# Attention and SwiGLU FFN on one core: Q and K by DMA transpose, weights over SP and Pool, matmuls in column tiles

## The chip, the cores and the metric

The kernel runs on one core of a Trainium2 chip. The core has five engines that run side by side and meet at semaphores: PE (matmuls), DVE (vector operations), ACT (activation functions and copies), POOL (GpSimd) and SP (which here only issues DMAs). DMA transfers are issued from the queue of an engine and run on 16 DMA engines. Matmul results land in PSUM, all other tiles in SBUF. The metric is device time of one execution, in microseconds, as the median of several runs.

## The reference, cut to what matters

Inputs are `q`, `k`, `v` of shape (8 batches, 12 heads, 448 positions, 64), the weights `w_gate` and `w_val` (768, 1536), `w_out` (1536, 768) and `rms_g` (768), all float32.

```python
scores = (q @ k.T) / sqrt(64)                 # per batch and head
attn   = maximum(scores, 0.0) ** 2 / 448
x      = (attn @ v)                           # heads side by side: (3584, 768)
rms = sqrt(mean(x * x, axis=-1) + 1e-06)
xn  = x / rms * rms_g
out = (silu(xn @ w_gate) * (xn @ w_val)) @ w_out
```

There is no softmax: a score is clipped at zero and squared, so nothing has to be summed over a row before the product with V.

## The kernel before, in words

Everything on PE is bfloat16 with float32 sums. All weights stay in SBUF. One batch of 448 positions is the unit of work, and the kernel keeps two in flight: while the FFN of batch b runs, the attention of batch b+1 is threaded into it.

Loading. Q, K and V of a batch come with the positions in four chunks of 112 partitions, cast from float32 to bfloat16 by the DMA itself, issued on POOL (`load`, L90). The weights come the same way (`load_w` L100, `load_wo` L107), behind the first batch's loads on the same queue.

Attention works on pairs of heads (`HP` = 6 pairs a batch). `transposes` (L154): DVE copies the pair's Q and K into order (`reorder`, L148, two copies), PE transposes eight 112x128 blocks into a PSUM tile `psT` (L163), and DVE copies that to SBUF as `qkT` (L169). `scores` (L182) multiplies, for each chunk of 112 keys, the two heads of the pair in two row tiles of the array (64 rows each); ACT clips at zero (L197), on every fourth chunk DVE (L195), and DVE squares (L198). `attend` (L207) multiplies the squares by V, the two heads of the pair into the two column halves of the array; ACT scales into `xT` (L215), DVE squares that into `x2` (L218). `psT` and `psAV` share one PSUM buffer.

The norm (`norm`, L235 to L255) sums `x2` over the features with a matmul by ones (`psSS`, L238), takes the square root on ACT (L243, another function table than Silu's), the reciprocal on DVE (L246), and multiplies six tiles of `xn` on DVE (L249).

The FFN (`ffn`, L305) of a batch has 12 blocks of 128 hidden features; each is a `gate` and a `value` unit of six 128x128 matmuls over 448 columns (L260), with Silu on ACT (L271) and the product `hT` on DVE (L277). Two batches together make seven tiles of 128 rows of output (`outproj`, L286): three at the end of an even batch, four at the end of an odd one, each in a part of 512 and a part of 256 columns, copied to SBUF by ACT (L293) and stored from SP (L300).

The order on every engine is the order in which the program issues, written out by hand: `merge` (L18) spreads the attention's units and the norm evenly over the first nine tenths of the FFN's units, by the weights that stand beside them. The first attention and norm run with nothing beside them. The last batch's FFN has no attention in it.

Of the kernel before, what the change touches and what calls it, by code (L numbers as in the profile page):

```python
# [8 lines left out]
FP32 = mybir.dt.float32  # L9
I32 = mybir.dt.int32  # L10
# [7 lines left out]
def merge(main, side, head=0.0, tail=0.0):  # L18


    total = sum(c for c, _ in main)
    if not main:
        return [f for _, f in side]
    out, done, k = [], 0.0, 0
    n = len(side)
    for c, f in main:
        while k < n and done >= total * (head + (1.0 - head - tail) * k / n):
            out.append(side[k][1])
            k += 1
        out.append(f)  # L30
        done += c
    out.extend(f for _, f in side[k:])
    return out
# [3 lines left out]
def kernel(  # L37
# [22 lines left out]
    NT = 2 * S // P  # L60

    ctx.enter_context(tc.manual_schedule())

    const = ctx.enter_context(tc.tile_pool(name="consts", bufs=1))
    wpool = ctx.enter_context(tc.tile_pool(name="weights", bufs=1))
    ldpool = ctx.enter_context(tc.tile_pool(name="ld", bufs=2))
    tpool = ctx.enter_context(tc.tile_pool(name="tsb", bufs=2))
    apool = ctx.enter_context(tc.tile_pool(name="attn", bufs=10))
    xpool = ctx.enter_context(tc.tile_pool(name="xT", bufs=2))
    npool = ctx.enter_context(tc.tile_pool(name="norm", bufs=2))  # L70
    hpool = ctx.enter_context(tc.tile_pool(name="hT", bufs=2))
    spool = ctx.enter_context(tc.tile_pool(name="sig", bufs=3))
    opool = ctx.enter_context(tc.tile_pool(name="ostage", bufs=3))
    ps_s = ctx.enter_context(tc.tile_pool(name="ps_s", bufs=2, space=bass.MemoryType.PSUM))
    ps_a = ctx.enter_context(tc.tile_pool(name="ps_a", bufs=1, space=bass.MemoryType.PSUM))
    ps_m = ctx.enter_context(tc.tile_pool(name="ps_m", bufs=3, space=bass.MemoryType.PSUM))
# [7 lines left out]
    def alloc_ld(b):  # L84
        for nm in ("q", "k", "v"):
            ld[nm, b] = ldpool.tile([PC, H, NCH * D], BF16, name=nm + "b", tag=nm + "b")

    def load(nm, b, h0=0, h1=H):
        src = {"q": q, "k": k, "v": v}[nm]
        nc.gpsimd.dma_start(out=ld[nm, b][:, h0:h1, :], in_=head_rows(src, b, h0, h1))  # L90
# [4 lines left out]
    NSL = 4  # L95
    FS = F // NSL

    def load_w(which, s):
        dst, src = {"g": (wg_sb, moe_w_gate), "v": (wv_sb, moe_w_val)}[which]
        nc.gpsimd.dma_start(  # L100
            out=dst[:, :, s * FS : (s + 1) * FS],
            in_=src.rearrange("(kt p) f -> p kt f", p=P)[:, :, s * FS : (s + 1) * FS],
        )

    def load_wo(s, n):
        w = FT // n
        nc.gpsimd.dma_start(  # L107
            out=wo_sb[:, s * w : (s + 1) * w, :],
            in_=moe_w_out.rearrange("(fk p) m -> p fk m", p=P)[:, s * w : (s + 1) * w, :],
        )  # L110

    alloc_ld(0)
    load("q", 0, 0, 2)
    load("k", 0, 0, 2)
    ident = const.tile([PC, PC], BF16, name="ident", tag="ident")
    masks.make_identity(nc, ident[:])
    ones_bf = const.tile([P, P], BF16, name="ones_bf", tag="ones_bf")
    nc.vector.memset(ones_bf[:], 1.0)
    eps_col = const.tile([P, 1], FP32, name="eps_col", tag="eps_col")
    nc.vector.memset(eps_col[:], eps)  # L120
    g_sb = wpool.tile([P, KT], FP32, name="g_sb", tag="rmsg")
    nc.sync.dma_start(out=g_sb[:], in_=moe_rms_g.rearrange("(kt p) -> p kt", p=P))
    load("q", 0, 2, 6)
    load("k", 0, 2, 6)
    load("v", 0, 0, 6)
    load("q", 0, 6, 12)
    load("k", 0, 6, 12)
    load("v", 0, 6, 12)
    for s in range(NSL):
        load_w("g", s)  # L130
        load_w("v", s)
        if s == 1:
            alloc_ld(1)
            load("q", 1)
            load("k", 1)
    load("v", 1)
    load_wo(0, 2)
    load_wo(1, 2)


    xTs = {}
    qkT = {}
    ldp = {}

    def reorder(b, j):
        for nm in ("q", "k"):
            t = tpool.tile([PC, NCH, 2, D], BF16, name=nm + "p", tag=nm + "p")
            nc.vector.tensor_copy(  # L148
                out=t[:].rearrange("p c h d -> p h c d"),
                in_=ld[nm, b][:, 2 * j : 2 * j + 2, :].rearrange("p h (c d) -> p h c d", c=NCH),  # L150
            )
            ldp[nm, b, j] = t

    def transposes(b, j):  # L154
        if j == 0:
            xTs[b] = xpool.tile([P, KT, S], BF16, name="xT", tag="xT")
            reorder(b, 0)
        if j + 1 < HP:
            reorder(b, j + 1)
        psT = ps_a.tile([P, 2, S], BF16, name="psT", tag="ps_a")  # L160
        for ti, nm in enumerate(("q", "k")):
            for c in range(NCH):
                nc.tensor.transpose(  # L163
                    out=psT[:, ti, c * PC : (c + 1) * PC],
                    in_=ldp[nm, b, j][:, c, :, :],
                    identity=ident[:],
                )
        t = tpool.tile([P, 2, S], BF16, name="qkT", tag="qkT")
        nc.vector.tensor_copy(out=t[:], in_=psT[:])  # L169
        qkT[b, j] = t  # L170

    rsq = {}
    state = {"n": 0}

    def scores(b, j, cs):
        t = qkT[b, j]
        pss = []
        for c in cs:
            psS = ps_s.tile([PC, 2, 512], FP32, name="psS", tag="psS")
            for hh in range(2):  # L180
                prt = slice(hh * D, (hh + 1) * D)
                nc.tensor.matmul(  # L182
                    out=psS[:, hh, :S],
                    lhsT=t[prt, 1, c * PC : (c + 1) * PC],
                    rhs=t[prt, 0, :],
                    start=True,
                    stop=True,
                )
            pss.append(psS)
        for c, psS in zip(cs, pss):  # L190
            r = apool.tile([PC, 2, S], BF16, name="r", tag="r")
            on_dve = state["n"] % 4 == 3
            state["n"] += 1
            if on_dve:
                nc.vector.tensor_relu(out=r[:], in_=psS[:, :, :S])  # L195
            else:
                nc.scalar.activation(out=r[:], in_=psS[:, :, :S], func=ACT.Relu)  # L197
            nc.vector.tensor_tensor(out=r[:], in0=r[:], in1=r[:], op=ALU.mult)  # L198
            rsq[b, j, c] = r

    x2s = {}

    def attend(b, j):
        psAV = ps_a.tile([P, S], FP32, name="psAV", tag="ps_a")
        for c in range(NCH):
            for hh in range(2):
# [6 lines left out]
                )  # L213
        xT = xTs[b]
        nc.scalar.mul(out=xT[:, j, :], in_=psAV[:], mul=inv_attn)  # L215
        if j == 0:
            x2s[b] = npool.tile([P, KT, S], BF16, name="x2", tag="x2")
        nc.vector.tensor_tensor(out=x2s[b][:, j, :], in0=xT[:, j, :], in1=xT[:, j, :], op=ALU.mult)  # L218

    def attention(b):  # L220
        units = [(0.4, lambda: transposes(b, 0))]
        for j in range(HP):
            units.append((0.5, lambda j=j: scores(b, j, (0, 1))))
            if j + 1 < HP:
                units.append((0.4, lambda j=j: transposes(b, j + 1)))
            units.append((0.5, lambda j=j: scores(b, j, (2, 3))))
            if j:
                units.append((0.8, lambda j=j: attend(b, j - 1)))
        units.append((0.8, lambda: attend(b, HP - 1)))
# [3 lines left out]
    xns, hTs = {}, {}  # L233

    def norm(b):  # L235
        psSS = ps_m.tile([P, S], FP32, name="psSS", tag="mm")
        for kt in range(KT):
            nc.tensor.matmul(  # L238
                out=psSS[:], lhsT=ones_bf[:], rhs=x2s[b][:, kt, :],
                start=(kt == 0), stop=(kt == KT - 1),  # L240
            )
        rstd = npool.tile([P, S], FP32, name="rstd", tag="rstd", bufs=1)
# [4 lines left out]
        xn = npool.tile([P, KT, S], BF16, name="xn", tag="xn")  # L247
        for kt in range(KT):
            nc.vector.scalar_tensor_tensor(  # L249
                out=xn[:, kt, :], in0=xTs[b][:, kt, :], scalar=g_sb[:, kt : kt + 1], in1=rstd[:],  # L250
                op0=ALU.mult, op1=ALU.mult,
            )
        xns[b] = xn
        if b % 2 == 0:
            hTs[b // 2] = hpool.tile([P, FT, 2 * S], BF16, name="hT", tag="hT")  # L255

    def project(w_sb, b, fb, nm):
        ps = ps_m.tile([P, S], FP32, name=nm, tag="mm")
        for kt in range(KT):
            nc.tensor.matmul(  # L260
                out=ps[:], lhsT=w_sb[:, kt, fb * P : (fb + 1) * P], rhs=xns[b][:, kt, :],
                start=(kt == 0), stop=(kt == KT - 1),
            )
# [10 lines left out]
    def value(b, fb):  # L274
# [3 lines left out]
            out=hTs[b // 2][:, fb, o : o + S], in0=sil[b, fb][:], in1=psV[:], op=ALU.mult  # L278
# [4 lines left out]
    def outproj(i, t, o, w):  # L283
        ps = ps_m.tile([P, 512], FP32, name="psO", tag="mm")
        for fk in range(FT):
            nc.tensor.matmul(  # L286
                out=ps[:, :w], lhsT=hTs[i][:, fk, t * P : (t + 1) * P], rhs=wo_sb[:, fk, o : o + w],
                start=(fk == 0), stop=(fk == FT - 1),
# [69 lines left out]
```

## Time and profile before

| | us |
|---|---|
| median of 3 runs (lowest, highest) | 548.66 (547.95, 550.68) |
| the profiled execution: span from its first to its last instruction | 544.9 |
| busy in it: PE, DVE, ACT, POOL | 485.1, 338.6, 252.3, 34.4 |

The profile is of one execution, and its own time is known as this span; the runs' median lies 3.8 us above it, which is what lies around the first and the last instruction. Busy times of PE include the modelled drain of a matmul, so two matmuls that follow each other overlap in it: what a matmul costs in a stream is read from the distance between starts.

### The profile page before, as it was taken

What the parts mean: (1) busy time and instruction counts of PE and PEld (TensorE: products, weight loads), DVE (VectorE), ACT (ScalarE), POOL (GpSimd) and SP (SyncE); (2) the same over time, 40 slices, a digit from 0 to 9 for tenths busy, and PEclk for the clock granted to TensorE, in tenths of its full rate; (3) what the DMA queues carried; (4) which work ended last, traced back from release to release, by engine and by line L of the source; (5) the groups of instructions that cost most, each with busy time, mean ns of one, the idle gap of its engine ahead of it and who ended that gap; (6) DMA issues with size and microseconds to landing.
All of it is one profiled execution on the core that took longest, in us unless ns stands there. A gap on an engine that the chain in (4) does not pass through costs nothing.

```text
span 544.9 us, 7394 instructions
## 1 busy us (share of the span) xinstructions
PE 485.1 (89%) x3024; PEld 236.1 (43%) x3024; DVE 338.6 (62%) x586; ACT 252.3 (46%) x369; POOL 34.4 (6%) x45
## 2 busy tenths in 40 slices
PE   3774999879999799888999799987999899989996
PEld 1331444434444344444444444444445444444553
DVE  3886677467764677566774677656775677745210
ACT  2553454524545354535444454454545445553221
POOL 7330001000010001000010000100000000000000
PEclk9976999979999899999999999999999999999999
DMA  9999938150073402560054500733001200002013
GB/s 114 201 201 205 203 53 102 35 103 1 1 102 73 95 1 24 79 123 16 1 75 86 108 1 1 103 58 80 1 1 29 78 10 2 1 29 59 0 30 88
DMA packets 45858, 35.08 MB, mean 64 GB/s; under 512 B 2304, under 2 KB 42240, under 8 KB 45824
## 3 DMA queue, kind: packets, MB, share of 16 engines
q0 software_dynamic: 40560, 23.60, 31.7%
q1 hardware_dynamic: 5264, 11.02, 6.8%
q8 instruction: 23, 0.38, 0.3%
q14 instruction: 11, 0.09, 0.1%
HBM read 47.19 MB, written 11.01 MB: 107 GB/s over the span
## 4 chain that ended last, share of the span: by engine, by line
PE 73%; DVE 14%; ACT 8%; issue 2%; DMA 1%; POOL 0%; ACTq 0%; POOLq 0%
PE psV L260 20%; PE psG L260 20%; PE psO L286 14%; PE psAV L207 8%; PE psS L182 8%; DVE xn L249 5%; DVE rstd L246 4%; ACT r L197 4%; PE psT L163 3%; ACT L243 2%; DVE r L198 2%; DVE r L195 1%; ACT rstd L243 1%; DMA kb<-in_k_dram 1%; ACT xT L215 1%
## 5 line engine op out<-in xcount | busy, mean ns | idle before, releaser
L198 DVE TENSOR_TENSOR r<-r 112x896 bf16<-112x896 bf16 x192 | 119.3, 625 | 93.8 <-ACT r L197 91.9
L197 ACT ACTIVATE r<-psS 112x896 bf16<-112x896 f32 x144 | 127.0, 916 | 52.5 <-PE psS L182 52.4
L260 PE MATMUL psG<-xn,wg_sb 128*128 128x448 bf16 x576 | 129.4, 360 | 1.1 <-DVE xn L249 1.0
L260 PE MATMUL psV<-xn,wv_sb 128*128 128x448 bf16 x576 | 128.0, 359 | 0.0
L286 PE MATMUL psO<-wo_sb,hT 128*128 128x512 bf16 (+1 forms) x672 | 115.2, 326 | 0.0
L271 ACT ACTIVATE sil<-psG 128x448 bf16<-128x448 f32 x96 | 52.3, 545 | 102.2 <-PE psG L260 90.8
L277 DVE TENSOR_TENSOR hT<-sil,psV 128x448 bf16<-128x448 bf16 x96 | 59.4, 618 | 45.9 <-PE psV L260 37.8
L286 PEld LDWEIGHTS <-hT 128*128 128x128 bf16 x672 | 63.6, 98 | 49.2 <-issue 9.3
L182 PE MATMUL psS<-qkT 64*112 64x448 bf16 x384 | 64.5, 394 | 19.3 <-ACT r L197 7.4
L260 PEld LDWEIGHTS <-wg_sb 128*128 128x128 bf16 x576 | 53.0, 99 | 59.8 <-issue 19.2
L260 PEld LDWEIGHTS <-wv_sb 128*128 128x128 bf16 x576 | 52.3, 99 | 57.5 <-issue 19.2
L293 ACT COPY ost<-psO 128x512 f32<-128x512 f32 (+1 forms) x56 | 26.9, 480 | 81.4 <-PE psO L286 81.4
L195 DVE TENSOR_SCALAR r<-psS 112x896 bf16<-112x896 f32 x48 | 52.0, 1084 | 0.0
L207 PE MATMUL psAV<-r,vb 112*64 112x448 bf16 x384 | 47.7, 370 | 4.6 <-DVE qkT L169 3.8
L182 PEld LDWEIGHTS <-qkT 64*112 64x112 bf16 x384 | 21.1, 131 | 60.5 <-issue 55.2
L163 PE MATMUL psT<-ident,qp 112*128 112x112 bf16 x192 | 19.0, 226 | 29.6 <-DVE qp L148 29.6
L215 ACT ACTIVATE xT<-psAV 128x448 bf16<-128x448 f32 x48 | 26.1, 545 | 33.7 <-PE psAV L207 33.7
L163 PEld LDWEIGHTS <-qp 112*128 112x128 bf16 x192 | 14.0, 103 | 40.9 <-DVE qp L148 31.9
L207 PEld LDWEIGHTS <-vb 112*64 112x64 bf16 x384 | 19.1, 111 | 28.9 <-issue 21.4
L246 DVE RECIPROCAL rstd<-rstd 128x448 f32<-128x448 f32 x8 | 23.6, 2953 | 12.8 <-ACT rstd L243 12.8
L169 DVE COPY qkT<-psT 128x896 bf16<-128x896 bf16 x48 | 29.8, 620 | 2.3 <-PE psT L163 2.1
L249 DVE SCALAR_TENSOR_TENSOR xn<-xT,g_sb,rstd 128x448 bf16<-128x448 bf16 x48 | 29.3, 680 | 0.3
(39 smaller groups left out, 157.6 us busy)
## 6 DMA issues: line engine op xcount, KB each, us to landing
qb<-in_q_dram POOLq DMA_DIRECT2D x7, 672.0 KB, 7.3
kb<-in_k_dram POOLq DMA_DIRECT2D x7, 672.0 KB, 9.8
vb<-in_v_dram POOLq DMA_DIRECT2D x7, 672.0 KB, 8.1
out_dram<-ost SPq DMA_DIRECT2D x8, 336.0 KB, 2.8
wg_sb<-in_moe_w_gate_dram POOLq DMA_DIRECT2D x4, 576.0 KB, 20.2
wv_sb<-in_moe_w_val_dram POOLq DMA_DIRECT2D x4, 576.0 KB, 21.8
wo_sb<-in_moe_w_out_dram POOLq DMA_DIRECT2D x2, 1152.0 KB, 28.3
out_dram<-ost SPq DMA_DIRECT2D x8, 288.0 KB, 5.3
```

The source lines that it names most:

```text
L163: nc.tensor.transpose(out=psT[:, ti, c * PC : (c + 1) * PC], in_=ldp[nm, b, j][:, c, :, :], identity=ident[:],)
L182: nc.tensor.matmul(out=psS[:, hh, :S], lhsT=t[prt, 1, c * PC : (c + 1) * PC], rhs=t[prt, 0, :], start=True, stop=True,)
L195: nc.vector.tensor_relu(out=r[:], in_=psS[:, :, :S])
L197: nc.scalar.activation(out=r[:], in_=psS[:, :, :S], func=ACT.Relu)
L198: nc.vector.tensor_tensor(out=r[:], in0=r[:], in1=r[:], op=ALU.mult)
L207: nc.tensor.matmul(out=psAV[hh * D : (hh + 1) * D, :], lhsT=ld["v", b][:, 2 * j + hh, c * D : (c + 1) * D], rhs=rsq[b, j, c][:, hh, :], st ...
L246: nc.vector.reciprocal(out=rstd[:], in_=rstd[:])
L249: nc.vector.scalar_tensor_tensor(out=xn[:, kt, :], in0=xTs[b][:, kt, :], scalar=g_sb[:, kt : kt + 1], in1=rstd[:], op0=ALU.mult, op1=ALU.mult,
L260: nc.tensor.matmul(out=ps[:], lhsT=w_sb[:, kt, fb * P : (fb + 1) * P], rhs=xns[b][:, kt, :], start=(kt == 0), stop=(kt == KT - 1),)
L271: nc.scalar.activation(out=s[:], in_=psG[:], func=ACT.Silu)
L277: nc.vector.tensor_tensor(out=hTs[b // 2][:, fb, o : o + S], in0=sil[b, fb][:], in1=psV[:], op=ALU.mult)
L286: nc.tensor.matmul(out=ps[:, :w], lhsT=hTs[i][:, fk, t * P : (t + 1) * P], rhs=wo_sb[:, fk, o : o + w], start=(fk == 0), stop=(fk == FT - 1),)
```

## The change

Six things change together.

1. Q and K. Batches 0 and 1 are still transposed on PE, now straight from the loaded tile, without the DVE reorder, each head to its own column half (16 narrow transposes for 8), into the PSUM buffers of the FFN. Batches 2 to 7 are reordered by DVE in half batches (three pairs) and transposed by a DMA from SP, issued during the FFN of the batch two before. Loads of Q and K have one buffer for two before.
2. Weights. SP fetches them as float32 in 18 slices into seven staging tiles, beginning when the last K load of batch 0 has landed; POOL casts them.
3. FFN, out-projection and statistics matmuls are each split into two of 64 output columns (`halves`).
4. Order. `spread` places units in stretches of the FFN. The squares stand apart from the scores. Batch 0's FFN has no out-projection; attention(1) begins at 0.45 of it and runs beyond its end, and norm(1) follows with nothing beside it. Batch 1's FFN gets all seven out tiles. The norm is split, and Silu's table is loaded by a one-element Silu behind the square root.
5. The DVE clip comes on the last chunk of every other pair from batch 2 on; the 256-column out copies go from ACT to DVE. The scores' stationary operand is 128 columns wide instead of 112 (16 unused).
6. Warm-up matmuls on zeros, before and during the first attention and norm.

The core of the diff:

```diff
-    def reorder(b, j):
-        for nm in ("q", "k"):
-            t = tpool.tile([PC, NCH, 2, D], BF16, name=nm + "p", tag=nm + "p")
...
+    def cast_w(which, s):
...
+        nc.gpsimd.tensor_copy(out=dst, in_=src)
...
+    def reorder(b, half):
+        t = late["kqp"].tile([PC, 2, NCH, HH, D], BF16, name="kqp", tag="kqp")
+        for ti, nm in enumerate(("k", "q")):
+            nc.vector.tensor_copy(
+                out=t[:, ti].rearrange("p c h d -> p h c d"),
+                in_=ld[nm, b][:, half * HH : (half + 1) * HH, :].rearrange(
+                    "p h (c d) -> p h c d", c=NCH
+                ),
+            )
+    def dma_transposes(b, half):
+        t = late["kqT"].tile([P, 2, NCH, JH, PC], BF16, name="kqT", tag="kqT")
+        nc.sync.dma_start_transpose(
+            out=t[:].rearrange("p t c j s -> p (t c j) s"),
+            in_=src[:].rearrange("p t c h d -> p (t c h d)"),
+        )
...
+    def halves(ps, w, lhsT, rhs, start, stop):
+        for hf in range(2):
+            prt = slice(hf * HALF, (hf + 1) * HALF)
+            nc.tensor.matmul(out=ps[prt, :w], lhsT=lhsT[:, prt], rhs=rhs, start=start, stop=stop)
...
+        nc.scalar.activation(out=warm_act[:], in_=eps_col[:], func=ACT.Silu)
...
+        warm(12)
+        for n, fn in enumerate(attention(0, True, lambda j: (3,))):
+            fn()
+            if n % 3 == 2:
+                warm(2)
+        norm_stat(0)
+        warm(14)
+        norm_apply(0)
...
+        ahead(4)
+        alloc_ld(1)
+        for nm in ("q", "k", "v"):
+            load(nm, 1)
...
+        for fn in spread(main, [(0.45, 1.3, attention(1, True, lambda j: (3,)))]):
+            fn()
+        ahead(len(order))
+        norm_stat(1)
+        norm_apply(1)
...
+        if b == 1:
+            main += out_tiles(0, 0, NT)
...
+        if b == 1:
+            prep = [lambda: prepare(2, 0), lambda: prepare(2, 1), lambda: fetch(3)]
+            spans.append((0.25, 0.3, prep))
+            spans.append((0.42, 0.84, attention(2, False, lambda j: (3,) if j % 2 else ())))
+        elif b + 1 < B:
+            spans.append((0.0, 0.80, attention(b + 1, False, lambda j: (3,) if j % 2 else ())))
         if b + 1 < B:
+            spans.append((0.86, 0.9, [lambda b=b: norm_stat(b + 1)]))
+            spans.append((0.90, 0.95, [lambda b=b: norm_apply(b + 1)]))
         if b + 2 < B:
+            prep = [lambda b=b: prepare(b + 2, 0), lambda b=b: prepare(b + 2, 1)]
+            if b + 3 < B:
+                prep.append(lambda b=b: fetch(b + 3))
+            spans.append((0.5, 0.7, prep))
```

`ahead(n)` casts the next slices up to the n-th and, for each, fetches the slice seven further on; it is called with 4 before batch 1's loads and then from step to step of batch 0's FFN. `prepare` is a half batch's reorder and transpose, `fetch` the loads of a batch.

## Rows read from the trace of the kernel before

**Rows 1.** The page: busy us (share) xinstructions, and the granted clock in 40 slices.

```profile
PE 485.1 (89%) x3024; PEld 236.1 (43%) x3024; DVE 338.6 (62%) x586; ACT 252.3 (46%) x369; POOL 34.4 (6%) x45
...
PEclk9976999979999899999999999999999999999999
```

**Rows 2.** The page: the chain that ended last, by engine.

```profile
PE 73%; DVE 14%; ACT 8%; issue 2%; DMA 1%; POOL 0%; ACTq 0%; POOLq 0%
```

**Rows 3.** The chain in order of time, 246 to 311: start us, us, what.

```profile
246.55 1.14 PE psG L260 x6
...
248.82 0.52 PE psS L182 x4
...
250.58 0.40 PE psT L163 x8
...
256.79 1.24 PE psG L260 x6
...
262.45 0.88 PE psAV L207 x8
263.33 1.24 PE psG L260 x6
...
306.37 3.67 DVE xn L249 x6
```

**Rows 4.** Timeline, all engines, 299 to 316: start, us, engine, line, [idle before].

```profile
300.75 0.87 PEld L238 LDWEIGHTS <-ones_bf 128*128 128x128 bf16 x6 [0.36 <-issue]
...
302.07 5.37 PE L286 MATMUL psO<-wo_sb,hT 128*128 128x256 bf16 x36
...
310.30 0.37 PE L163 MATMUL psT<-ident,qp 112*128 112x112 bf16 x4 [2.86 <-DVE qp L148]
```

**Rows 5.** Timelines of one attend, 484.04 to 484.2 and 484.2 to 484.4.

```profile
484.05 0.14 PEld L207 LDWEIGHTS <-vb 112*64 112x64 bf16 x4 [0.21 <-issue]
484.05 0.38 PE L207 MATMUL psAV<-r,vb 112*64 112x448 bf16 x2
...
484.05 0.57 PE L207 MATMUL psAV<-r,vb 112*64 112x448 bf16 x4
```

**Rows 6.** Timeline, last batch's four out tiles.

```profile
523.95 15.67 PEld L286 LDWEIGHTS <-hT 128*128 128x128 bf16 x96
```

**Rows 7.** Groups by line and form: xcount | busy us, mean ns | idle before.

```profile
L198 DVE TENSOR_TENSOR r<-r 112x896 bf16<-112x896 bf16 x192 | 119.3, 625 | 93.8 <-ACT r L197 91.9
...
L260 PEld LDWEIGHTS <-wg_sb 128*128 128x128 bf16 x576 | 53.0, 99 | 59.8 <-issue 19.2
...
L195 DVE TENSOR_SCALAR r<-psS 112x896 bf16<-112x896 f32 x48 | 52.0, 1084 | 0.0
...
L169 DVE COPY qkT<-psT 128x896 bf16<-128x896 bf16 x48 | 29.8, 620 | 2.3 <-PE psT L163 2.1
...
L207 PEld LDWEIGHTS <-vb 112*64 112x64 bf16 x384 | 19.1, 111 | 28.9 <-issue 21.4
...
L148 DVE COPY kp<-kb 112x512 bf16<-112x512 bf16 x48 | 14.1, 293 | 1.0 <-DMA kb<-in_k_dram 1.0
...
L218 DVE TENSOR_TENSOR x_245<-xT 128x448 bf16<-128x448 bf16 x6 | 2.3, 389 | 1.3 <-ACT xT L215 1.3
```

**Rows 8.** The chain in order of time, first 60 us.

```profile
41.07 2.19 PE psSS L238 x6
...
51.80 2.24 PE psG L260 x6
```

**Rows 9.** Timeline, all engines, 0 to 12.

```profile
3.02 0.27 POOL masks.py:199 TENSOR_SCALAR_AFFINE_SELECT ident<-ident 112x112 bf16<-112x112 bf16 x1
...
8.60 0.29 DVE L148 COPY kp<-kb 112x512 bf16<-112x512 bf16 x1 [0.79 <-DMA kb<-in_k_dram]
8.81 0.62 DVE L169 COPY qkT<-psT 128x896 bf16<-128x896 bf16 x1
```

**Rows 10.** The page: DMA queue, packets, MB, share of 16 engines' span.

```profile
q0 software_dynamic: 40560, 23.60, 31.7%
```

More of the change, by code (lines that the diff above doesn't have):

```diff
@@ L15, with spread @@
 NCH = 4
-def merge(main, side, head=0.0, tail=0.0):
+def spread(main, spans):
     total = sum(c for c, _ in main)
-    if not main:
-        return [f for _, f in side]
+    placed = []
+    for lo, hi, units in spans:
+        n = len(units)
+        placed += [(total * (lo + (hi - lo) * i / max(n, 1)), f) for i, f in enumerate(units)]
+    placed.sort(key=lambda x: x[0])
     out, done, k = [], 0.0, 0
-    n = len(side)
     for c, f in main:
-        while k < n and done >= total * (head + (1.0 - head - tail) * k / n):
-            out.append(side[k][1])
+        while k < len(placed) and done >= placed[k][0] - 1e-9:
+            out.append(placed[k][1])
             k += 1
@@ L154, in transposes @@
[L154 to L161, printed above, removed]
-            for c in range(NCH):
[L163 to L168, printed above, removed]
+    stage = {}
@@ new lines, in pe_transposes @@
+    def pe_transposes(b, j):
+        psT = ps_m.tile([P, 2, S], BF16, name="psT", tag="mm")
+        for ti, nm in enumerate(("k", "q")):
+            for c in range(NCH):
+                for hh in range(2):
+                    nc.tensor.transpose(
+                        out=psT[hh * D : (hh + 1) * D, ti, c * PC : (c + 1) * PC],
+                        in_=ld[nm, b][:, 2 * j + hh, c * D : (c + 1) * D],
+                        identity=ident[:],
+                    )
+        t = late["qkT"].tile([P, 2, S], BF16, name="qkT", tag="qkT")
@@ L222, in attention @@
         for j in range(HP):
[L223 to L226, printed above, removed]
+            dv = dve_chunks(j)
+            units.append(lambda j=j, dv=dv: scores(b, j, (0, 1), dv))
             if j:
-                units.append((0.8, lambda j=j: attend(b, j - 1)))
-        units.append((0.8, lambda: attend(b, HP - 1)))
@@ L230, in attention @@
-        return units
-    xns, hTs = {}, {}
-    def norm(b):
+                units.append(lambda j=j: squares(b, j - 1, (2, 3)))
+            if by_pe and j + 1 < HP:
+                units.append(lambda j=j: pe_transposes(b, j + 1))
+            units.append(lambda j=j, dv=dv: scores(b, j, (2, 3), dv))
+            units.append(lambda j=j: squares(b, j, (0, 1)))
+            if j:
+                units.append(lambda j=j: attend(b, j - 1))
+        units.append(lambda: squares(b, HP - 1, (2, 3)))
@@ L259, in project @@
         for kt in range(KT):
[L260 to L263, printed above, removed]
+            halves(ps, S, w_sb[:, kt, fb * P : (fb + 1) * P], xns[b][:, kt, :], kt == 0, kt == KT - 1)
         return ps
@@ new lines @@
+    alloc_ld(0)
+    load("q", 0, 0, 2)
+    load("k", 0, 0, 2)
+    ident = const.tile([PC, PC], BF16, name="ident", tag="ident")
+    masks.make_identity(nc, ident[:])
+    ones_bf = const.tile([P, P], BF16, name="ones_bf", tag="ones_bf")
+    nc.vector.memset(ones_bf[:], 1.0)
+    eps_col = const.tile([P, 1], FP32, name="eps_col", tag="eps_col")
+    nc.vector.memset(eps_col[:], eps)
+    warm_act = const.tile([P, 1], FP32, name="warm_act", tag="warm_act")
+    nc.scalar.activation(out=warm_act[:], in_=eps_col[:], func=ACT.Sqrt)
@@ new lines, with warm @@
+    warm_in = const.tile([P, S], BF16, name="warm_in", tag="warm_in")
+    nc.vector.memset(warm_in[:], 0.0)
+    g_sb = wpool.tile([P, KT], FP32, name="g_sb", tag="rmsg")
+    nc.sync.dma_start(out=g_sb[:], in_=moe_rms_g.rearrange("(kt p) -> p kt", p=P))
+    load("q", 0, 2, 6)
+    load("k", 0, 2, 6)
+    load("v", 0, 0, 6)
+    load("q", 0, 6, 12)
+    last_k = load("k", 0, 6, 12)
+    load("v", 0, 6, 12)
+    def warm(n):
+        ps = ps_a.tile([P, S], FP32, name="psW", tag="ps_a")
+        for _ in range(n):
+            nc.tensor.matmul(out=ps[:], lhsT=warm_in[:, :P], rhs=warm_in[:], start=True, stop=True)
@@ new lines, in name_of, with ahead, stepped, step @@
+    def name_of(i):
+        return (i.ins if hasattr(i, "ins") else i)
+    with tc.tile_pool(name="stage", bufs=7) as sp, tc.tile_pool(name="qkT", bufs=2) as tp:
+        late["stage"], late["qkT"] = sp, tp
+        order = []
+        for s in range(NSL):
+            order += [("g", s), ("v", s)]
+        order += [("o", s) for s in range(FT // 2)]
+        first = fetch_w(*order[0])
+        tc.add_manual_dep(
+            name_of(first),
+            name_of(last_k).name,
+            mybir.DependencyInfo(mybir.DependencyClass.Sync, mybir.DependencyReason.DATA),
+            reason="weights after the first batch",
+        )
+        for w in order[1:7]:
+            fetch_w(*w)
+        warm(12)
[6 more added lines that the diff above has]
+        norm_apply(0)
+        fed = [0]
+        def ahead(n):
+            while fed[0] < min(n, len(order)):
+                cast_w(*order[fed[0]])
+                if fed[0] + 7 < len(order):
+                    fetch_w(*order[fed[0] + 7])
+                fed[0] += 1
+        ahead(4)
+        alloc_ld(1)
+        for nm in ("q", "k", "v"):
+            load(nm, 1)
+        def stepped(n, f):
+            def step():
+                ahead(n // 2 + 4)
+                f()
+            return step
+        main = [(c, stepped(n, f)) for n, (c, f) in enumerate(gate_value(0))]
+        for fn in spread(main, [(0.45, 1.3, attention(1, True, lambda j: (3,)))]):
[3 more added lines that the diff above has]
+        norm_apply(1)
@@ new lines, with prepare, fetch @@
+    late["kqp"] = pool("kqp", 2)
+    late["kqT"] = pool("kqT", 3)
+    late["hpool"] = pool("hT1")
+    def prepare(b, half):
+        reorder(b, half)
+        dma_transposes(b, half)
+    def fetch(b):
+        alloc_ld(b)
+        for nm in ("q", "k", "v"):
+            load(nm, b)
+    fetch(2)
+    full = S // P
+    for b in range(1, B):
+        main = gate_value(b)
+        if b == 1:
+            main += out_tiles(0, 0, NT)
+        elif b % 2 == 0:
+            main += out_tiles(b // 2, 0, full)
+        else:
+            main += out_tiles(b // 2, full, NT)
+        spans = []
+        if b == 1:
[4 more added lines that the diff above has]
+            spans.append((0.0, 0.80, attention(b + 1, False, lambda j: (3,) if j % 2 else ())))
```

218 lines of the change are left out of this document (104 added, 114 removed).

## The prediction

> **What bounds the kernel now.** I read the busy table and the clock strip first [rows 1]: PE is busy for 485.1 of 544.9 us, DVE for 338.6, and the granted clock is full (2.4 GHz) from about the fifth slice on. The chain that ended last says the same: 73% of it is PE, 14% DVE, 8% ACT [rows 2]. The chain in order of time over one batch shows where DVE gets in [rows 3]. Through the body of a batch nearly every link is a PE group: a gate or value group of six 448-column matmuls takes 1.14 us (0.19 us a matmul), a scores unit 0.52, a transposes unit 0.40, an attend 0.88. After scores or attend the next group shows 1.24, so a change of array tile costs some 0.10 us on the way back. Towards the end of the batch the chain leaves PE for the norm, whose last link is the six xn (3.67). The timeline there [rows 4] shows why: PE has out-projection until 307.44, then sits idle for 2.86 us until a q reorder, which DVE holds behind the xn, lets the next batch's first transpose go. So the batches are PE-bound with one bubble each. The first 50 us are another regime: one attention alone, which goes at DVE's pace.
>
> The sum is made on the profiled span, 544.9 us; the median of the runs is 3.8 us more, and I add that at the end.
>
> **FFN in column tiles.** Each matmul becomes two of 64 output columns, so a pair must cost what one did. Nearest row: attend already works so. Two of its matmuls end within 0.38 us, four within 0.57 [rows 5], so a pair adds 0.19 us, exactly the full-width price; two that did not overlap would need 0.38. I take 0. In the 256-column half of an out tile there is less to hide a weight load behind: a tile takes 15.67 / 4 = 3.9 us [rows 6], of which 12 x 0.217 = 2.6 is the 512-column half, so a narrow matmul takes 0.108 us. Four 64-column loads lie within 0.14 us [rows 5], a pair in 0.07 to 0.14: 0 to 32 ns on 336 narrow pairs, 0 to +11 us; I take 3 ns, **+1**, since in the row the loads overlap. The Trainium skill (TensorEngine Tiling, Restrictions and Gotchas) says that column tiling disables Fast Weight Load. A 64-column load of attend takes 111 ns against 99 for a 128-column one of the FFN [rows 7], so the trace agrees. By that rule alone, two loads of 111 ns one after the other in place of 108, a narrow pair would lose 114 ns and the sum 38 us; the four loads in 0.14 us speak against it.
>
> What column tiles buy is that attend, statistics and FFN share one array tile. An attend costs 0.88 + 0.10, its four pairs 4 x 0.19 = 0.76: 0.22 x 6 an iteration x 6 = **-7.9**. Scores stay row-tiled and keep 0.52 + 0.10. (Bounds: 0, were the 0.22 drain rather than switch, to -7.9.)
>
> **Q, K of batches 2 to 7 by DMA transpose.** Six units of 0.40 leave PE in each of iterations 1 to 6: **-14.4**. On DVE the six qkT copies (0.62) go and the reorder stays, in four copies of 1536 elements, 3 x 0.29 = 0.9 us each by its row [rows 7]: 3.5 us, as before. DVE loses 3.7 us an iteration, and 3.2 more as the DVE relu comes only in every other pair; it gains about 1.4 with the narrow out copies. So DVE falls from 42 to some 37 us, ACT rises from 31.5 to 33, both under PE's 57 or so: these edits cost nothing while that holds.
>
> The transposes are covered by lead. From iteration 2's data on, they are issued in the middle of the iteration before, some 25 us ahead of first use; for batch 2 at 0.25 of iteration 1 against a use at 0.42, about 9 us. No row shows a DMA transpose. Each carries 0.69 MB. Below: the queue's mean rate of 200 GB/s in the early slices would be 3.4 us. Above: the software queue's 40560 packets took 31.7% of 16 engines over 544.9 us [rows 10], 68 ns each; cut in 128-byte pieces the transfer is 5376 of them, 5376 x 68 ns / 16 = 23 us. I take 9, at which neither lead is used up: 0; at 23 only the first is short, by some 14. SP waits in order: behind a transpose stand only stores of out tiles, with three staging tiles; in iteration 1 the second pair is issued just as out tiles begin, 0 to +5 there, taken as 0. The Trainium skill says of the same thing, in Advanced Engine Details and Errata (X-Bar Transpose), about the speed of plain copies, and in VectorE: DVE Perf Modes (the three transpose paths), 1309 ns for a 128x128; 24 such blocks in series would be an estimated 31 us. No run here shows either; it belongs to the third rival.
>
> **The bubble.** Nothing of the next batch waits on a reorder any more, since scores(0) of two batches on read tiles that landed long ago. What is late next is xn: from the start of the statistics matmuls to the last xn is 300.75 to 310.04, 9.3 us [rows 3, 4], plus 0.4 for an out copy now on DVE between. PE has 1.14 + 1.3 + 3.9 + 0.62 = 7.0 us of work, then a first gate group that must wait for its last xn piece: 9.7 + 0.2 against 7.0 + 1.14. 1.5 us remain of 2.86: **-8** over six batches (bounds 0 and -17).
>
> **Early in a batch** PE loses about 1.1 us: 246.55 to 256.79 is 10.2 us for six FFN groups, three scores units and one transposes unit, 6 x 1.14 + 3 x 0.62 + 0.40 = 9.1 [rows 3]. Silu's table now loads right behind Sqrt, and the first pair has no DVE relu: I take 0.7 back, **-4** over six (0 to -7).
>
> **The first 118 us.** Per head pair DVE has two reorders, one qkT copy, four squares, one relu, one x2: 2 x 0.29 + 0.62 + 4 x 0.625 + 1.08 + 0.39 = 5.17 us [rows 7], and six of them, 31.0, are the 31.6 us from the first scores at 9.5 to the statistics at 41.07 [rows 8, 9]. Without the reorders it is 4.59, 27.5 for six. The first qkT copy stood behind the second reorder, which waited for its load until 8.6; now it follows its transposes, after 12 warm-up matmuls of 0.373 from 1.4: scores at about 7.4. Statistics at 7.4 + 27.5 + 0.6 = 35.5. From there to the first gate group: 51.80 + 2.24 - 41.07 = 13.0 before, at half clock; warm, and with no transposes between, 8.5 + 0.2, so 44.2 instead of 54.0.
>
> Then the filler moves. Gate and value of batch 0 run alone for 10 more groups, 11.4 us, to 55.6; 13 groups (14.8) with 23 of the 36 units of attention(1), 3.8 pairs at 2.5 us of PE, to 79.9; the other 2.2 pairs stand alone at DVE's 4.6, to 90; the norm with nothing beside it, 9.5, to 99.5. Before, the first gate group of batch 1 was done at 118.5 with three out tiles (11.7) done as well, which now come later: 106.8 to compare. **-7**: most of the prologue's ten is given back, since batch 1's norm has lost its cover.
>
> Pool's 18 casts of 1536 elements a partition: nearest rows 0.27 us for 112 elements on Pool [rows 9], 3.8 us each by that, and 0.9 by DVE's copy [rows 7]. I take 2.5; 4 before batch 1's loads, which wait for the last transposes of batch 0 at 31 us, the rest 34 to 70. A slice pair serves two blocks, 4.5 us, so even 3.8 keeps the weights ahead: 0. While DVE is the pace, casts may get in its way: bounds 0 and, six to eight casts of 2.5 on the path, +18; taken **+4**, near the lower end, as half of DVE's time there is on PSUM. The tail (batch 7) is unchanged.
>
> **Sum.** 1 - 7.9 - 14.4 - 8 - 4 - 7 + 4 = -36.3; 508.6 span, plus 3.8: 512.4, say **512**.
>
> **Rivals.** (1) Pool holds DVE up: each square and xn that falls on a cast waits for it, first in pairs 3 to 6 of attention(0), then in norm(0) and attention(1). Price 6 to 8 casts, +14 over my 4: 518 to 530. For: DVE sets the pace there; against: later casts fall where FFN alone runs. The Trainium skill (SBUF, the shared port pair) has it as an exclusive lock against DVE operations with two SBUF inputs; no run here shows that. (2) A column pair costs 200 to 220 ns for 190, through four instructions where there were two: 1152 gate and value pairs by 10 to 30 ns: +12 to +35, 524 to 547. For: no row has a long run of pairs; against: four pairs of attend go at 0.19, and transposes issue 16 instructions in 0.40, faster than a pair needs. (3) Transposes come late and the kernel is slower. Place: scores at the head of each iteration, PE waiting for kqT. An iteration takes 63 us now (544.9 less 118.5 and less the last batch's own 47, which are 23 x 1.14, 15.7 and a tail of 5 [rows 6], over six) and about 57 in my sum, and two transposes per iteration go one after the other: beyond 28 us each they set the iteration, and from about 32 each, 64 an iteration, all of the gain is gone. At 64-byte pieces, 46 us each: 92 an iteration against 57, +35 x 6, some 722. For: no row for the operation; against: even 128-byte pieces give 23. (4) The fill lost in iterations 0 and 1 costs more, PE at half clock behind the bare norm and tiles stalled behind SP: +20 to +35, 532 to 547.
>
> **Chances.** Mine 0.64 (496 to 526), rivals 0.17, 0.07, 0.07, 0.05. The low end is mine with both stalls gone whole (-9 and -3) and nothing for Pool (-4); the high end takes in rival 1 and the lower halves of 2 and 4: 493 to 536. A run tells a change from none at 0.5%, 2.7 us. Faster by that: 0.90; slower: 0.08 (rival 3 and a little of 2 and 4); between, 0.02.
>
> **What would show it.** Right: FFN groups of twelve at 1.14 to 1.2; an attend followed by a group at 1.14; no PE transposes after about 90 us; PE's wait before a batch's first gate named xn, about 1.5 us; DMA transposes landing in under 20 us; iterations 2 to 6 of 54 to 60 us; the first gate near 44, batch 1's near 100. Wrong: PE waits named kqT; group times over 1.25; DVE squares or xn stretched while Pool casts; PE idle on weights.

## The result, and the profile after

| | before | after |
|---|---|---|
| median of the runs, us (lowest, highest) | 549.67 (547.95, 551.34) | 518.93 (515.89, 519.9) |
| span of the profiled execution, us | 544.9 | 514.1 |

The ratio after to before is 0.944, with a 95% interval of 0.940 to 0.948; 512 us was forecast, with a range of 493 to 536. The page of the kernel after, for [rows 1, 2]:

```profile
PE 476.3 (93%) x4754; PEld 264.8 (52%) x4754; DVE 301.0 (59%) x489; ACT 256.2 (50%) x367; POOL 53.8 (10%) x53
...
PEclk8887799959999999999999999999999999999999
...
PE 76%; DVE 14%; issue 5%; ACT 3%; DMA 1%; POOL 0%; DVEq 0%; ACTq 0%; POOLq 0%
```

The kernel is more PE-bound than before, but the clock is lower at the start: it is under full in the first five slices (64 us), and about half in the ninth (103 to 116 us). The chain in order of time, for [rows 3], in an iteration and at its end:

```profile
205.40 0.76 PE psAV L209 x8
206.15 1.14 PE psV L251 x12
...
230.34 1.17 DVE r L202 x2
...
231.54 0.38 PE psAV L209 x2
...
240.26 3.66 DVE xn L268 x6
...
243.96 0.38 PE psG L251 x2
```

An attend takes 0.76 and the group after it 1.14, no transposes are left, and one PE piece follows the other until the last attend, which waits for its squares, and the first gate group, which waits for xn. The squares from 44 us on, for [rows 7] (duration in ns: shortest, median, longest), and the start of the chain, for [rows 8]:

```profile
L202 DVE TENSOR_TENSOR r<-r x168: 613/618/620, 75.8 to 454.2; 112x896 bf16<-112x896 bf16 x168
```

```profile
44.79 2.31 PE psSS L251 x7
...
56.29 2.24 PE psV L251 x12
...
113.61 0.58 PE psG L251 x2
```

The statistics of batch 0 start at 44.8 (41.1 before), its first gate group ends at 56.3 (54.0 before), that of batch 1 at 114.2. The mean of a square has gone from 625 to 657 ns, and all of the rise lies in the first 45 us: the 168 later squares take at most 620 ns, the first 24 up to 3289 (shown with the first experiment).

Where the 30.8 us of span came from, and what was forecast for each stretch. The stretches end where a first gate group ends, in the kernel before and after:

```profile
118.49 2.24 PE psV L260 x6
...
497.85 0.35 PE psG L260
```

```profile
467.24 0.38 PE psG L251 x2
```

| stretch | before | after | difference | forecast |
|---|---|---|---|---|
| to the end of batch 1's first gate group, less 11.7 for three out tiles where they are done by then | 106.8 | 114.2 | +7.4 | -3 |
| from there to the end of batch 7's first gate group, the three tiles put back | 391.2 | 353.4 | -37.8 | -33.3 |
| the rest of batch 7 | 46.9 | 46.5 | -0.4 | 0 |

So the time lies within the range, 6.9 us above the forecast, and two errors of opposite sign stand behind it: the start lost 10.4 us against the forecast, and the batches gained 4.5 more than I said.

### The profile page after: what moved, and what is told of

It is laid out like the page before. It is cut to its first block, busy times and chain, and to the rows that moved or that the text cites. A ratio compares the mean times of both kernels' runs of the same rounds, so it can differ in the third digit from the quotient of the medians.

```text
span 514.1 us, 10918 instructions
## 1 busy us (share of the span) xinstructions
PE 476.3 (93%) x4754; PEld 264.8 (52%) x4754; DVE 301.0 (59%) x489; ACT 256.2 (50%) x367; POOL 53.8 (10%) x53
## 4 chain that ended last, share of the span: by engine, by line
PE 76%; DVE 14%; issue 5%; ACT 3%; DMA 1%; POOL 0%; DVEq 0%; ACTq 0%; POOLq 0%
PE psV L251 22%; PE psG L251 22%; PE psO L251 16%; PE psS L187 8%; PE psAV L209 6%; DVE xn L268 5%; DVE r L202 5%; DVE rstd L262 2%; PE psSS L251 2%; DVE r L194 1%; ACT r L196 1%; DMA kb<-in_k_dram 1%; PE psT L142 1%; PE psW L368 1%; ACT xT L220 1%
## 5 line engine op out<-in xcount | busy, mean ns | idle before, releaser
L251 PE MATMUL psG<-xn,wg_sb 128*64 128x448 bf16 x1152 | 136.6, 360 | 13.5 <-DVE xn L268 13.3
L251 PE MATMUL psV<-xn,wv_sb 128*64 128x448 bf16 x1152 | 128.3, 357 | 0.0
L251 PE MATMUL psO<-wo_sb,hT 128*64 128x512 bf16 (+1 forms) x1344 | 115.4, 326 | 0.0
L251 PEld LDWEIGHTS <-wg_sb 128*64 128x64 bf16 x1152 | 67.8, 110 | 70.1 <-issue 34.9
L251 PEld LDWEIGHTS <-hT 128*64 128x64 bf16 x1344 | 77.9, 110 | 33.6 <-issue 4.0
L251 PEld LDWEIGHTS <-wv_sb 128*64 128x64 bf16 x1152 | 67.5, 111 | 47.2 <-issue 12.8
L312 ACT COPY ost<-psO 128x512 f32<-128x512 f32 x28 | 16.4, 585 | 60.5 <-PE psO L251 56.0
L187 PE MATMUL psS<-kqT 64*128 64x448 bf16 x288 | 40.8, 354 | 3.0 <-ACT r L196 1.5
L221 DVE TENSOR_TENSOR x<-xT 128x448 bf16<-128x448 bf16 x48 | 19.2, 401 | 40.5 <-ACT xT L220 40.4
L194 DVE TENSOR_SCALAR r<-psS 112x896 bf16<-112x896 f32 x30 | 32.6, 1086 | 7.1 <-PE psS L187 7.1
L187 PE MATMUL psS<-qkT 64*128 64x448 bf16 x96 | 16.4, 392 | 5.6 <-ACT r L196 3.3
## 6 DMA issues: line engine op xcount, KB each, us to landing
wst<-in_moe_w_val_dram SPq DMA_DIRECT2D x6, 768.0 KB, 11.7
```

The source lines that it names most:

```text
L187: nc.tensor.matmul(out=psS[:, hh, :S], lhsT=flat[:, o : o + P], rhs=rhs, start=True, stop=True)
L194: nc.vector.tensor_relu(out=r[:], in_=psS[:PC, :, :S])
L251: nc.tensor.matmul(out=ps[prt, :w], lhsT=lhsT[:, prt], rhs=rhs, start=start, stop=stop)
```

## The experiments

Each was timed against the kernel before, whose medians in these sittings were 548.4 to 550.5 us; ratios are to it, with their 95% intervals. All start from the kernel after unless another is named.

**Weights cast by the DMA.**

```diff
-        first = fetch_w(*order[0])
...
-        for w in order[1:7]:
-            fetch_w(*w)
+        for w in order[:12]:
+            load_cast(*w)
...
-        ahead(4)
         alloc_ld(1)
         for nm in ("q", "k", "v"):
             load(nm, 1)
+        for w in order[12:]:
+            load_cast(*w)
```

`load_cast` is a `gpsimd.dma_start` from float32 to bfloat16, as before the change.

> The changed kernel with one part undone: the weights are cast by the DMA itself from POOL's queue, as before the change; no staging, no casts on Pool. Theory (Pool's casts hold DVE): squares in the first attention go back from 21.3 us busy to about 14, the statistics matmuls start near 36 instead of 44.8, the first gate group ends near 47 instead of 56.1, and the time falls from 519 to 507 to 511. Rival (the start is set by loads, ACT or the clock, and the stretched squares only fill idle time): statistics at 43 or later, time 516 to 520. Second rival (weights and batch 1's loads in one queue come late): squares short, but PE or DVE waits on a load appear in batch 0, time 514 or more.

Measured: 507.23 us, ratio 0.925 (0.920 to 0.930). One line's instructions in the first 56 and 50 us (duration min/median/max in ns), of the kernel after and of this one, and this one's chain:

```profile
L202 DVE TENSOR_TENSOR r<-r x24: 607/617/3289, 12.5 to 42.0; 112x896 bf16<-112x896 bf16 x24
```

```profile
L212 DVE TENSOR_TENSOR r<-r x24: 612/616/619, 11.3 to 33.0; 112x896 bf16<-112x896 bf16 x24
```

```profile
35.17 1.27 PE psSS L261 x12
...
44.23 1.14 PE psV L261 x12
...
99.98 2.24 PE psV L261 x12
```

The theory holds. No square is longer than 619 ns, the statistics start at 35.2, the first gate group ends at 44.2 and that of batch 1 at 100.0. The forecast's working without Pool had 35.5, 44.2 and 99.5. So the start comes out as forecast, and undoing the casts is worth 11.7 us. The edit also removes the float32 fetches and their staging; that it is the casts that stretch the squares is shown by the next run, which changes them alone. Of the 14.2 us gained by the end of batch 1's first gate group 11.5 are left in the span: 1.0 goes in the next iteration, where PE now waits for batch 2's transposed half (1.6 us), and 1.7 in batch 7, where two of the first groups take 2.24 and 1.48 us.

**Casts in pieces.**

```diff
-        nc.gpsimd.tensor_copy(out=dst, in_=src)
+        for i in range(dst.shape[1]):
...
+                nc.gpsimd.tensor_copy(out=dst[:, i, :], in_=src[:, i, :])
```

A piece has 256 elements a partition, and a cast has six pieces.

> The changed kernel with each cast on Pool cut into six of 256 elements a partition. Theory A (a DVE operation waits until the running Pool instruction has ended): a square waits for at most some 0.3 us a piece, so the longest square falls from 3.29 us to under 1.5, the 7.5 us of excess on the first attention's squares to under 4, and the time from 519 to 513 to 516. Theory B (Pool and DVE share a rate, whatever the length of an instruction): the excess stays at 6 to 9 us, time 518 to 521. If each piece costs Pool some 0.1 us more, the casts end later but still ahead of the FFN.

Measured: 519.19 us, ratio 0.942 (0.935 to 0.949): no change in time. Two lines' instructions in the first 50 and 62 us:

```profile
L207 DVE TENSOR_TENSOR r<-r x24: 614/808/841, 12.4 to 37.2; 112x896 bf16<-112x896 bf16 x24
```

```profile
L273 DVE SCALAR_TENSOR_TENSOR xn<-xT,g_sb,rstd x6: 809/810/6512, 46.3 to 55.6; 128x448 bf16<-128x448 bf16 x6
```

On the squares theory A holds, though not in the time: the longest falls from 3289 to 841 ns, the line's busy time in the first 44.8 us from 21.3 to 16.4 (13.7 without casts), and the statistics start at 40.2 instead of 44.8. But the gain is given back in the norm: one xn stands 6.51 us while some 18 short casts (6.51 / 0.35) pass behind each other, and the first gate group ends at 57.1, later than in the kernel after (56.3). Timelines of 46.2 to 52.7 and 52.7 to 56:

```profile
46.25 7.25 DVE L273 SCALAR_TENSOR_TENSOR xn<-xT,g_sb,rstd 128x448 bf16<-128x448 bf16 x2
46.97 2.11 POOL L130 CAST wg_sb<-wst 128x256 bf16<-128x256 f32 x6
49.04 2.11 POOL L130 CAST wv_sb<-wst 128x256 bf16<-128x256 f32 x6
...
52.82 3.52 PE L256 MATMUL psG<-xn,wg_sb 128*64 128x448 bf16 x10 [6.64 <-DVE xn L273]
```

So here the length of a Pool instruction bounded the wait only while the two engines took turns, as they did on the squares and on the other five xn (0.81 us each). Why they did not on this one is open.

**Whole tiles again.**

```diff
-        for hf in range(2):
-            prt = slice(hf * HALF, (hf + 1) * HALF)
-            nc.tensor.matmul(out=ps[prt, :w], lhsT=lhsT[:, prt], rhs=rhs, start=start, stop=stop)
+        nc.tensor.matmul(out=ps[:, :w], lhsT=lhsT, rhs=rhs, start=start, stop=stop)
```

> The changed kernel with FFN, out-projection and statistics matmuls whole again (128 output columns), attend still in column halves. Theory (what column tiles buy is the change of array tile around attend): attend with what follows goes from 0.75 to about 0.98 us again, 0.22 x 36 in the batches under an FFN: 526 to 528 instead of 519; an FFN group and an out tile cost the same. Rival A (column halves change nothing that counts): 518 to 520. Rival B (column halves cost a little in weight loads that the profile hides): under 518.

Measured: 527.80 us, ratio 0.962 (0.958 to 0.966): 8.9 us slower, as the theory has it. Its chain:

```profile
260.96 1.14 PE psV L249 x6
262.09 0.88 PE psAV L209 x8
262.97 1.24 PE psG L249 x6
```

The 0.22 us around an attend is back, and it was a change of tile, not a drain of attend itself: in the kernel after, the same eight matmuls take 0.76 and the next group 1.14. With attention(1) there are up to 42 such attends under an FFN, an estimate of 9.2 us. The Trainium skill (TensorEngine Tiling (Array Packing), Key Properties) says that changing the tiling mode drains the engine; the trace agrees, at 0.12 us on the way in and 0.10 on the way out.

**Batch 0's out tiles given back.**

```diff
-        for fn in spread(main, [(0.45, 1.3, attention(1, True, lambda j: (3,)))]):
...
+        main += out_tiles(0, 0, S // P)
+        spans = [(0.20, 0.82, attention(1, True, lambda j: (3,)))]
+        spans.append((0.86, 0.9, [lambda: norm_stat(1)]))
+        spans.append((0.90, 0.95, [lambda: norm_apply(1)]))
+        for fn in spread(main, spans):
             fn()
-        ahead(len(order))
-        norm_stat(1)
-        norm_apply(1)
...
-            main += out_tiles(0, 0, NT)
+            main += out_tiles(0, full, NT)
```

> The changed kernel with three out tiles of batch 0 given back to batch 0's FFN, attention(1) spread from 0.20 to 0.82 of that, norm(1) at 0.86 and 0.90 as in the other batches; batch 1 keeps four tiles. Theory (the bare tail of attention(1) and the bare norm(1) cost what they leave PE idle, some 10 us, and a cold clock after): first gate group of batch 1 with three out tiles done at about 116 instead of 114.2 without them, time 519 to 507 to 511. Rival (attention(1) is then stretched by the casts on Pool and by PSUM buffers, and the gain is given back in batch 0): 515 to 520.

Measured: 509.85 us, ratio 0.930 (0.925 to 0.934), 9.1 us less. The first gate group of batch 1 ends at 115.8 with the three tiles done, against 114.2 without, and its next groups run at 1.14 where the kernel after has 1.66 for the first:

```profile
115.76 1.14 PE psV L251 x12
```

**Both.** The weights cast by the DMA and batch 0's out tiles back.

> Both edits together: weights cast by the DMA, and the three out tiles of batch 0 back under attention(1) and norm(1). Theory (two separate losses, one before 56 us, one between 93 and 115): the gains of 11.7 and 9.1 us add up, 519 to 497 to 500. Rival (both edits remove the same idle stretch, since attention(1) also ran beside casts): 502 to 507.

Measured: 495.50 us, ratio 0.902 (0.897 to 0.907). The two losses are separate; together they are 23.4 us, a little more than 11.7 + 9.1; why more is not shown. One wait grows, to 4.7 us: that for batch 2's first transposed half, whose lead the second edit shortens.

**All batches transposed on PE.**

```diff
-            spans.append((0.0, 0.80, attention(b + 1, False, lambda j: (3,) if j % 2 else ())))
+            spans.append((0.0, 0.80, attention(b + 1, True, lambda j: (3,) if j % 2 else ())))
...
-            prep = [lambda b=b: prepare(b + 2, 0), lambda b=b: prepare(b + 2, 1)]
```

> The changed kernel with Q and K of batches 2 to 7 transposed on PE as those of batches 0 and 1 are (16 narrow transposes a pair, one DVE copy), no DVE reorder, no DMA transpose, Q and K with two buffers from batch 2 on. Theory (the DMA transpose takes 0.39 to 0.40 us a pair off a PE that is the bound): 36 x 0.4 = 14.4 us more, 519 to 532 to 535. Rival A (part of it hides in the waits that iterations still have): 522 to 529. Rival B (the transposes' PSUM tile takes a buffer from the FFN's three and holds its groups up as well): 537 or more.

Measured: 545.77 us, ratio 0.994 (0.991 to 0.998): 26.8 us slower than the kernel after, near the kernel before, so rival B's size. But the trace names another place than PSUM. Chain at the head of a batch:

```profile
247.02 3.65 DVE xn L269 x6
...
251.00 0.54 DVE qkT L149
...
251.59 0.80 PE psS L188 x4
252.40 2.38 PE psV L252 x12
254.78 0.64 PE psT L143 x16
255.42 1.14 PE psG L252 x12
```

The first pair's qkT copy stands behind xn on DVE, and scores wait for it. From 247.8 to 251.0 PE is busy for 2.20 of 3.20 us, and then its next group runs at the lower clock: 2.38 us for 1.14 to 1.26, with a granted clock of 0.50 from 252.4 to 254.8.

**The first transposes ahead of the norm**, from that kernel.

```diff
-            spans.append((0.0, 0.80, attention(b + 1, True, lambda j: (3,) if j % 2 else ())))
+            spans.append((0.0, 0.80, attention(b + 1, True, lambda j: (3,) if j % 2 else ())[1:]))
+        if b + 2 < B:
+            spans.append((0.84, 0.86, [lambda b=b: pe_transposes(b + 2, 0)]))
```

> The kernel with all batches transposed on PE, with one edit: the first pair's transposes of the batch after next are issued at 0.84 of an iteration, ahead of the norm, instead of at the head of the next one. Theory (of the 27 us that PE transposes cost over the changed kernel, 14.4 are PE's own time and most of the rest is the first qkT copy, which stands behind xn on DVE and leaves PE idle and its clock halved at the head of six batches): 546 to 533 to 537. Rival (the rest comes from the transposes' use of the FFN's PSUM buffers throughout): 543 to 547.

Measured: 533.78 us, ratio 0.971 (0.965 to 0.978). So of the 26.8 us 12.0 were the queue on DVE and the clock behind it, on average 2.4 at each of the five heads that the edit changes (batches 3 to 7); the granted clock had fallen to 0.50 at three of them. 14.9 remain, and 36 units of 0.40 are 14.4 of them, so next to nothing is left for PSUM.

```profile
247.03 0.38 PE psG L252 x2
247.41 0.39 PE psT L143 x16
247.81 1.14 PE psV L252 x12
```

**No warm-up.** All calls of `warm` left out.

> The changed kernel without its warm-up matmuls (12 at the start, 2 after every third unit of the first attention, 14 in the first norm). Theory (the first attention goes at DVE's pace, and the clock falls to its lower level anyway after 30 us): 517 to 521, with the first scores 1 us earlier and the first gate groups cold as they are now. Rival A (the warm-ups keep PE's small pieces off the chain): 522 to 527, statistics matmuls starting 3 us or more later. Rival B (they delay the attention's matmuls in PE's order): 513 to 516.

Measured: 514.31 us, ratio 0.937 (0.932 to 0.942). That lies 4.6 us under the kernel after and in the range of rival B, but the intervals of the two ratios overlap, so I call it no loss rather than a gain. The statistics start 1.5 us earlier (43.3), no xn is stretched by a cast, and the clock comes back sooner. Granted clock from 50 to 60 us, without warm-up and with it (columns: stretch, length, PE busy, clock, DMA, GB/s):

```profile
50.00:60.00 10.00, 9.84 (x78) 0.78 1.18 305
```

```profile
50.00:60.00 10.00, 6.61 (x34) 0.68 1.18 307
```

**Norm earlier, alone.**

```diff
-            spans.append((0.0, 0.80, attention(b + 1, False, lambda j: (3,) if j % 2 else ())))
+            spans.append((0.0, 0.76, attention(b + 1, False, lambda j: (3,) if j % 2 else ())))
-            spans.append((0.86, 0.9, [lambda b=b: norm_stat(b + 1)]))
-            spans.append((0.90, 0.95, [lambda b=b: norm_apply(b + 1)]))
+            spans.append((0.80, 0.9, [lambda b=b: norm_stat(b + 1)]))
+            spans.append((0.85, 0.95, [lambda b=b: norm_apply(b + 1)]))
```

In iteration 1 attention ends at 0.79 instead of 0.84.

> The changed kernel with one edit: from batch 1 on, attention ends by 0.76 (0.79 in iteration 1) of an iteration, and the norm stands at 0.80 and 0.85 instead of 0.86 and 0.90. Theory (at the head of each batch PE loses some 2 us to xn and to the last squares, which more lead removes; of the 14.4 us between the two last versions the rest is batch 2's transposes, 4.7, and batch 1's norm): 8 to 12 us less, 519 to 507 to 511. Rival (only the named waits go, 0.9 us in each of six): 512 to 515.

Measured: 506.09 us, ratio 0.921 (0.915 to 0.928), 12.8 us less: about 2.1 us a batch. Its chain at the end of the same iteration:

```profile
228.69 0.76 PE psAV L209 x8
229.45 1.31 PE psO L251 x24
230.76 1.14 PE psSS L251 x12
231.90 7.80 PE psO L251 x96
239.70 0.31 PE psS L187 x2
...
240.85 0.92 ACT r L196
```

xn and the squares are gone from it; what is last at the head of the batch now is ACT, whose two clips take 1.7 us.

**All three edits**, with attention(1) from 0.15 to 0.78, its norm at 0.80 and 0.85, and in iteration 1 batch 2's transposes at 0.10 and its attention from 0.36.

> Both edits together, and the attention ends by 0.76 of an iteration instead of 0.80, the norm stands at 0.80 and 0.85 instead of 0.86 and 0.90, batch 2's transposes are issued at 0.10 of iteration 1. Theory (xn is what is late at the start of a batch, some 0.9 us in each of six, and batch 2's transposes some 2): 5 to 8 us under the kernel with both edits, 490 to 494. Rival (attention pressed into less of the FFN waits for ACT and its two PSUM buffers and gives it back): 496 to 501.

Measured: 481.13 us, ratio 0.878 (0.873 to 0.883), 14.4 us under the kernel with two edits, twice what I expected: I had counted only the waits that the list of waits names, 0.9 us a batch for xn.

**The same without warm-up.**

> The fastest version so far (weights cast by the DMA, batch 0's out tiles back, attention and norm earlier) without any warm-up matmul. Theory (without casts on Pool the first attention goes at DVE's pace, and PE needs its full clock there only for the first gate groups): 1 to 3 us slower or equal, 480 to 485, the first one or two gate groups at 2.2 instead of 1.14. Rival (as in the changed kernel, warm-ups only stand in PE's order): 476 to 479.

Measured: 480.81 us, ratio 0.874 (0.870 to 0.879): no difference. Its statistics and first value group run at the lower clock (2.20 and 2.21 against 1.27 and 1.14; the granted clock is 0.64 from 33.8 to 46.0), but the statistics start 2.6 us earlier. These two are the fastest versions, and this one lies 12.6% under the kernel before and 7% under the changed one.

## Why the prediction held, point by point

The time lies in my band (496 to 526) and at the edge of rival 1's (518 to 530), and the mechanism of rival 1 is there too. That it stayed in mine is in part luck: the batches gave back some of what the start lost. And the low end of the range, 493, does not follow from its terms: 9 + 3 + 4 off 512 is 496.

**Column tiles: right.** Groups of twelve take 1.14, pairs run side by side. The tax on narrow halves (+1) is not there: in the chain the last four out tiles take 15.61 us against 15.62 before. The saving around attend was put at 7.9 and measures 8.9.

**DMA transposes: right.** 14.4 was forecast, 14.9 measured between the kernel after and the one with PE transposes early. The trace has the issue on SP (ns: shortest, median, longest) and the time to landing:

```profile
L166 SPq DMA_TRANSPOSE kqT<-kqp x12: 3187/3324/9707, 128.9 to 391.5; - x12
...
DMA to landing us min/median/max: 5.0/8.0/18.7
```

9 us was taken. Rival 3 is refuted: in the steady iterations the first transpose is issued 22 to 26 us ahead of its first use (218.4 and 240.8, for one). Only batch 2's lead, 10 us, was short: its first scores start at 138.75 after 1.3 us in which PE stands idle, and the first four transposes take 13.9 us to landing in the median.

**The head of a batch: near in sum, in parts that I had wrong.** 8 + 4 were forecast for taking DVE's queue off the head of a batch. The 12.0 by which the two kernels with PE transposes differ is not a measure of them, since it holds what the clock lost at three heads of the slower one. By subtraction, the 37.8 that the batches gained less 8.9 for tiles and 14.9 for transposes leave 14.0 for heads and bodies, where 8 + 4 - 1 were forecast. Some 2 of the 3 us between may be clock that I had not priced. In that stretch the kernel before has three groups that run below full clock, the two shown here and the one at 118.49, and the kernel after has one (1.66); by their excess over 1.14 that is an estimate of 1.1 + 1.1 + 0.45 - 0.5.

```profile
183.28 2.24 PE psG L260 x6
185.52 1.59 PE psV L260 x6
```

What is left at a head was said to be 1.5 us of xn; the forecast's own terms, 9.7 + 0.2 less 7.0 + 1.14, give 1.8. From the start of the narrow out half at 229.06, PE has 1.31 for that half, 0.76 of attend, 2.6, 1.14, 5.2 of out tiles, 0.48 and 1.14, which is 12.6 us, up to 244.34: some 2.7 are lost, 1.9 to xn, and 0.8 to the last attend, whose squares come late on DVE. That wait I had not seen.

**The start: wrong in one term.** The forecast's +4 for Pool's casts is the step that failed. Against the kernel with casts by DMA the end of batch 1's first gate group lies 14.2 us later (114.2 and 100.0), and the run 11.7 us. The mechanism was the first rival's, and its price, 14 over my 4, is nearer than mine. I took the low end because half of DVE's time is on PSUM. The trace shows one square over nearly two casts:

```profile
33.40 4.14 DVE L202 TENSOR_TENSOR r<-r 112x896 bf16<-112x896 bf16 x2
33.77 1.88 POOL L125 CAST wv_sb<-wst 128x1536 bf16<-128x1536 f32 x1
35.60 1.46 POOL L125 CAST wg_sb<-wst 128x1536 bf16<-128x1536 f32 x1
```

Two squares that take 1.15 us elsewhere take 4.14 here. The casts were shorter than assumed (1.46 to 1.88 us, 2.5 taken) and stood about where I had them: eight from 20.3 to 40.2 us, over the last four pairs, and later ones over an xn. It was the price of meeting one that was wrong. Part of the 14.2 is the clock: while PE waited for xn it fell, and the two groups after the first gate group took 2.24 and 2.18 us, at a granted clock of 0.50 and 0.54.

Not all of it lies under a cast. One stretched square has only Pool's issues of batch 1's loads beside it:

```profile
30.03 1.92 DVE L202 TENSOR_TENSOR r<-r 112x896 bf16<-112x896 bf16 x1
...
30.50 0.93 POOL L95 DMA_DIRECT2D kb<-in_k_dram  x1
```

In the kernel with casts by DMA squares over such issues take at most 619 ns, so it is not the issues alone; what held this one is open.

The Trainium skill (SBUF — State Buffer, Who interferes with whom) says that a DVE operation with two SBUF inputs and a Pool operation that reads SBUF block each other for a whole instruction. The squares of the kernel with short pieces agree with it (at most 841 ns); the xn that stood through some 18 casts is longer than one instruction would explain.

**The fill: right.** The filler that batch 1's norm lost was priced inside the -7, and without casts the stretch came out to half a microsecond; giving it back is worth 9.1 us. Rival 4 priced the same loss a second time and is refuted.

## What to carry to other kernels

Before work is moved to an idle engine, look at whose operations stretch beside it while they are on the chain: 28 us of casts on an idle Pool (10.1, 9.0 and 8.8 by line) cost 12 us of a kernel that had DMA to spare for them. In an order written by hand, the first operation of a batch on each queue must not stand behind the last of the one before: in the kernel with PE transposes that one queue position was worth 12.0 us, the transposes themselves 14.9. And a list of waits undercounts: where work is merely thin before a wait, take the stretch from end to end and subtract the work in it.

## What the runs showed of the hardware that I had not expected

- A DVE operation can stand for much longer than one Pool instruction: 3.29 us over casts of 1.47, and 6.51 us through some 18 casts of 0.35.
- The clock column at the very start is not to be trusted. Without warm-up it shows 1.00 from 10 to 20 us, while four matmuls of scores there take 0.93 us together; in the body of the kernel after, where it also shows full, four take 0.55:

```profile
9.87 0.93 PE L187 MATMUL psS<-qkT 64*128 64x448 bf16 x4
...
10.00:20.00 10.00, 8.79 (x72) 1.00 1.12 213
```

```profile
200.71 0.55 PE L187 MATMUL psS<-kqT 64*128 64x448 bf16 x4
```
